# Wider first weight rows in contraction halves, with eight gate blocks of two columns held open in PSUM

## The chip, the cores and the metric

The kernel runs on one core of a Trainium2 chip. The metric is device time in microseconds (us) of one execution. Before the change the median is 178.38 us over six runs (178.31 to 178.41). The profiled execution of the kernel before was taken apart from the six, and took 178.62 us, and its span (first to last instruction) is about 1.7 us shorter than its device time.

Names: PE is the matrix engine and PEld its weight loads, DVE the vector engine, ACT the scalar engine, SP the engine that issues most transfers. Times "at 6.66" are us from the start of the span.

## The reference, cut to what matters

```python
# x [1, 2048, 512], w_gate and w_up [512, 1792], w_down [1792, 512], all bf16
xn = _layernorm(x, axis=-1)
A = irfft2(rfft2(xn) * (w_r + 1j * w_i))             # spectral branch
g = einsum("bsd,df->bsf", xn, w_gate)                # contraction over 512
u = einsum("bsd,df->bsf", xn, w_up)
B = einsum("bsf,fd->bsd", gelu(g) * u, w_down)
return x + A + B
```

The change touches only the first 14 us: loading x and the first columns of `w_gate` and `w_up`, and the first matmuls of g and u.

## The kernel before

The 2048 rows of x are 16 "columns" c of 128 rows. The 1792 columns of the weights are 14 blocks "fc" of 128. The contraction of 512 is four blocks e of 128. A "unit" computes gate and up for n columns and m blocks fc. For columns 0 and 1 the kernel wants to start before all weights are there, so its transfers and units are cut finely. The order of instructions is decided by a planner from keys and estimated times (`add(engine, duration, function, dependences, key=...)`).

The loads, in their order in the queue:

```python
pin(load_x(0, 1))                      # column 0 of x, 128 KB
pin(load_x(1, 1))
nc.sync.dma_start(out=idx_t[:], ...)   # a small index table, needed much later
load_w(Wg_sb, 0, 512)                  # 512 KB: fc 0-3, all four e; rows of 512 bf16 = 1 KB
load_w(Wu_sb, 0, 512)                  # 512 KB
load_x(2, 2)
for e in range(0, NE, 2):
    load_w(Wg_sb, 512, 1024, e=slice(e, e + 2))   # fc 4-7, two e at a time
load_w(Wu_sb, 512, 1024)
load_x(4, 4)
load_w(Wg_sb, 1024, DF)
...
```

Before the weights are there, PE spins: 37 matmuls of no use at the start, and 11 more after the transposes of column 0, meant to keep its clock up.

```python
for k in range(37):
    pin(nc.tensor.matmul(sp_ps[:, :P], lhsT=spin[:], rhs=spin[:], start=True, stop=True))
def spin_on():
    for k in range(11):
        nc.tensor.matmul(sp_ps[:, :P], lhsT=spin[:], rhs=x_t[:, 0, :P], start=True, stop=True)
```

The first units, `(first column, columns, first fc, fc)`, and the piecewise gate of the first of them:

```python
todo = [(0, 1, 0, 4), (1, 1, 0, 4), (0, 2, 4, 2), (0, 2, 6, 2)]
todo += [(2, 2, f, 2) for f in range(0, 8, 2)]
...
def mm_part(e0, e1):
    if e0 == 0:
        b["g_ps"] = ps.tile([P, m, w], F32, name="g_ps", tag="G", bufs=2)
    for e in range(e0, e1):
        for f in range(m):
            T_.matmul(b["g_ps"][:, f], lhsT=Wg_sb[:, e, (f0 + f) * P:(f0 + f + 1) * P],
                      rhs=rhs[:, e, :], start=(e + f == 0), stop=(e == NE - 1), ...)
...
if k == 0:
    g = add("PE", occ / 4, lambda: mm_part(0, 1), [xT_op[0, 0]], key=1000, ...)
    between["t", 0].deps.append(g)           # transposes of column 1 between the parts
    g = add("PE", occ / 4, lambda: mm_part(1, 2), [g, between["t", 1]], key=1000.1)
    g = add("PE", occ / 2, lambda: mm_part(2, NE), [xT_op[0], g], key=1000.2, ...)
```

So for fc 0 to 3 a landed piece of 512 KB feeds gate (or up) of column 0 and of column 1 over the whole contraction.

Of the kernel before, what the change touches and what calls it, by code (L numbers as in the profile page):

```python
# [10 lines left out]
P = 128  # L11
BF16 = mybir.dt.bfloat16
F32 = mybir.dt.float32
# [4 lines left out]
S = 2048  # L18
# [3 lines left out]
NE = 4  # L22
# [112 lines left out]
class Plan:  # L135
# [6 lines left out]
    def add(self, eng, occ, fn, deps=(), key=0.0, lat=None, slack=0.0, t_min=0.0, acq=(), rel=(), after=None):  # L142
        lat = occ + 0.25 if lat is None else lat
        op = Op(len(self.ops), eng, occ, lat, fn, [d for d in deps if d is not None], key, slack, t_min, acq, rel,
                after)
        self.ops.append(op)
        return op
# [54 lines left out]
def kernel(  # L202
# [24 lines left out]
    ps = ctx.enter_context(tc.tile_pool(name="ps", bufs=2, space=bass.MemoryType.PSUM))  # L227
    pw = ctx.enter_context(tc.tile_pool(name="pw", bufs=2))
# [3 lines left out]
    Wg_sb = pc.tile([P, NE, DF], BF16, name="Wg_sb")  # L232
    Wu_sb = pc.tile([P, NE, DF], BF16, name="Wu_sb")
# [19 lines left out]
    def load_x(c0, n, eng=nc.sync):  # L253
        eng.dma_start(out=x_t[:, c0:c0 + n, :], in_=x_v[:, c0:c0 + n, :])

    def load_w(a, b, eng=nc.sync):
        nc.sync.dma_start(out=Wg_sb[:, :, a:b], in_=wg_v[:, :, a:b])
        eng.dma_start(out=Wu_sb[:, :, a:b], in_=wu_v[:, :, a:b])
# [23 lines left out]
    pin(load_x(1, 1))  # L282
    idx_t = pc.tile([P, 3], I32, name="idx_t")
    nc.sync.dma_start(out=idx_t[:], in_=nc.inline_tensor(idx_np, name="spec_rows").ap())
    load_w(Wg_sb, 0, 512)
    load_w(Wu_sb, 0, 512)
    load_x(2, 2)
    for e in range(0, NE, 2):
        load_w(Wg_sb, 512, 1024, e=slice(e, e + 2))
    load_w(Wu_sb, 512, 1024)  # L290
    load_x(4, 4)
    load_w(Wg_sb, 1024, DF)
    load_w(Wu_sb, 1024, DF)
    load_x(8, 2)
# [10 lines left out]
        for h in range(2):  # L305
            nc.sync.dma_start(out=Tf[64 * h:64 * h + 64, W:8 * W], in_=rows[h, :, 0:4, W:8 * W])

    LAND = {0: 2.7, 1: 3.4, 2: 8.55, 3: 8.55}
    LAND.update({c: 11.5 if c < 8 else 17.5 if c < 12 else 20.5 for c in range(4, NC)})
    WG_LAND = [6.1] * 4 + [10.15] * 4 + [13.2] * 6  # L310
    WU_LAND = [7.6] * 4 + [11.7] * 4 + [15.2] * 6
    RF_LAND = 19.0

    ident = ident_t[:]
# [5 lines left out]
        pin(nc.tensor.matmul(sp_ps[:, :P], lhsT=spin[:], rhs=spin[:], start=True, stop=True))  # L320

    def spin_on():
        for k in range(11):
            nc.tensor.matmul(sp_ps[:, :P], lhsT=spin[:], rhs=x_t[:, 0, :P], start=True, stop=True)

    plan = Plan({"S": 4, "G": 2, "U": 2, "ge": 3, "A": 1, "xf": 2, "ds": 4, "E": 2, "X": 2, "Y": 2, "F": 2,
                 "F2": 3, "y_sb": 3})
    add = plan.add
    V, A, T_ = nc.vector, nc.scalar, nc.tensor
# [18 lines left out]
    def f_T(c, e0, n):  # L348
        tiles["T", c, e0] = tp = ps.tile([P, n, P], BF16, name="tp", tag="S", bufs=4)
        for e in range(n):  # L350
            T_.transpose(tp[:, e], xn[:, c, (e0 + e) * P:(e0 + e + 1) * P], ident)  # L351
# [20 lines left out]
    xn_op, xT_op, between = {}, {}, {}  # L372

    def first_two():
        o = {}

        def v(k, fn, occ, deps=(), lat=None, t_min=0.0):
            o[k] = add("DVE", occ, fn, [o[d] for d in deps], key=-2000 + len(o), lat=lat, t_min=t_min,
                       after=o.get("last"))
            o["last"] = o[k]  # L380

        def T(c, h):
            o["T", c, h] = add("PE", 0.12, lambda: f_T(c, 2 * h, 2), [o["xn", c, h]], key=-2000 + 2 * c + h,
                               lat=0.36, acq=("S",))

        def xn_(c, h):
            v(("xn", c, h), lambda: f_norm_v(c, 256 * h, 256), 0.27, [("recip", c)], lat=0.4)

        def stats(c):
            v(("stats", c), lambda: f_stats(c), 0.6, t_min=LAND[c], lat=0.7)  # L390

        def mean(c):
            v(("mean", c), lambda: f_mean(c), 0.17, [("stats", c)])
            o["root", c] = add("ACT", 0.31, lambda: A.activation(
                out=rstd[:, c:c + 1], in_=mv[:, c, 1:2], func=AF.Sqrt, bias=eps_t[:], scale=1.0),
                [o["mean", c]], key=-2000 + c)

        def recip(c):
            v(("recip", c), lambda: V.reciprocal(out=rstd[:, c:c + 1], in_=rstd[:, c:c + 1]), 0.15, [("root", c)])

        stats(0)
        mean(0)
        stats(1)

        recip(0)
        xn_(0, 0)
        mean(1)
        xn_(0, 1)
        T(0, 0)
        T(0, 1)  # L410
        add("PE", 0.61, spin_on, [o["T", 0, 1]], key=-1500, lat=0.61, after=o["T", 0, 1])
        table = add("ACT", 1.3, lambda: None, [o["root", 1]], key=-1500, lat=1.3)
        v("copy0", lambda: f_Tc(0, 0, 2), 0.25, [("T", 0, 0)], lat=0.4)
        o["copy0"].rel = ("S",)
        xT_op[0, 0] = o["copy0"]
        recip(1)
        v("copy1", lambda: f_Tc(0, 2, 2), 0.25, [("T", 0, 1)], lat=0.4)
        o["copy1"].rel = ("S",)
        xT_op[0] = o["copy1"]
        xn_op[0] = o["xn", 0, 1]  # L420
        v("xn1", lambda: f_norm_v(1, 0, D), 0.33, [("recip", 1)], lat=0.45)
        o["t", 0] = add("PE", 0.12, lambda: f_T(1, 0, 2), [o["xn1"]], key=1000.04, lat=0.3, acq=("S",))
        o["t", 1] = add("PE", 0.12, lambda: f_T(1, 2, 2), [o["xn1"]], key=1000.05, lat=0.3, acq=("S",),
                        after=o["t", 0])
        between.update(o)
        v("copyt0", lambda: f_Tc(1, 0, 2), 0.25, [("t", 0)], lat=0.4)
        o["copyt1"] = add("ACT", 0.4, lambda: f_Tc(1, 2, 2, A.copy), [o["t", 1], table], key=-1400)
        o["copyt0"].rel = o["copyt1"].rel = ("S",)
        xT_op[1, 0] = o["copyt0"]
        xT_op[1] = o["copyt1"]  # L430
        xn_op[1] = o["xn1"]
# [42 lines left out]
    def unit(k, c0, n, f0, m=1):  # L474
        sb, o, w = c0 // 4, (c0 % 4) * P, n * P
# [10 lines left out]
        b = {}  # L486
# [7 lines left out]
                    T_.matmul(b[name][:, f], lhsT=W_[:, e, (f0 + f) * P:(f0 + f + 1) * P], rhs=rhs[:, e, :],  # L494
                              start=(e == 0), stop=(e == NE - 1))

        def mm_part(e0, e1):
            if e0 == 0:
                b["g_ps"] = ps.tile([P, m, w], F32, name="g_ps", tag="G", bufs=2)
            for e in range(e0, e1):  # L500
                for f in range(m):
                    T_.matmul(b["g_ps"][:, f], lhsT=Wg_sb[:, e, (f0 + f) * P:(f0 + f + 1) * P], rhs=rhs[:, e, :],  # L502
                              start=(e + f == 0), stop=(e == NE - 1), skip_group_check=True)

        def f_ge():
            b["ge"] = pw.tile([P, m, w], BF16, name="ge", bufs=3)
            A.activation(out=b["ge"][:], in_=b["g_ps"][:], func=AF.Gelu_apprx_tanh)  # L507

        def f_h():
# [6 lines left out]
        def split(name, tag, W_, key, t, h):  # L516
            o = None
            for f in range(0, m, h):
                o = add("PE", occ * h / m, lambda f=f: mm(name, tag, W_, range(f, f + h)), [o] if f else src, key=key,
                        lat=occ * h / m + 0.3, acq=() if f else (tag,), t_min=t[f0 + f + h - 1])  # L520
            return o

        if k == 0:
            g = add("PE", occ / 4, lambda: mm_part(0, 1), [xT_op[0, 0]], key=1000, acq=("G",), t_min=WG_LAND[0])
            between["t", 0].deps.append(g)
            g = add("PE", occ / 4, lambda: mm_part(1, 2), [g, between["t", 1]], key=1000.1)
            g = add("PE", occ / 2, lambda: mm_part(2, NE), [xT_op[0], g], key=1000.2, lat=occ / 2 + 0.3)
        elif k < 4:
            late_half = WG_LAND[f0] + 0.05
            first = [xT_op[1, 0]] if k == 1 else src  # L530
            g = add("PE", occ / 2, lambda: mm_part(0, 2), first, key=1000 + k if k < 3 else 1002.2, acq=("G",),
                    t_min=late_half - (0.7 if k > 1 else 0.0))
            g = add("PE", occ / 2, lambda: mm_part(2, NE), [*src, g], key=1000.3 + k, lat=occ / 2 + 0.3, t_min=late_half)
        else:
            g = split("g_ps", "G", Wg_sb, 1000 + k, WG_LAND, m)
        u = split("u_ps", "U", Wu_sb, (1001.4, 1001.5, 1003.1, 1003.5)[k] if k < 4 else 1000.5 + k, WU_LAND, (2, m, 1)[k] if k < 3 else m)
        ge = add("ACT", {1: 0.28, 2: 0.36, 4: 0.5}[n * m], f_ge, [g], key=-1000 + k,
                 lat={1: 0.38, 2: 0.48, 4: 0.7}[n * m], acq=("ge",), rel=("G",))
        h = add("DVE", {1: 0.21, 2: 0.34, 4: 0.61}[n * m], f_h, [ge, u], key=-1000 + k, rel=("U", "ge"))
        for c in range(c0, c0 + n):  # L540
            for f in range(f0, f0 + m):
                h_op[c, f] = h

    todo = [(0, 1, 0, 4), (1, 1, 0, 4), (0, 2, 4, 2), (0, 2, 6, 2)]
    todo += [(2, 2, f, 2) for f in range(0, 8, 2)]
    todo += [(0, 4, f) for f in range(8, NFC)]
    todo += [(4 * sb, 4, f) for sb in range(1, NSB) for f in range(NFC)]
# [345 lines left out]
```

## Time and profile before

| reading | value | view |
|---|---|---|
| device time | 178.38 us | timed runs |
| PE busy | 172.8 us, 98% | page, part 1 |
| share of the waiting chain that is PE | 95% | page, part 4 |
| first gate matmul | 6.66 | timeline |
| first 256-wide unit (columns 2-3) | 14.49 | timeline |
| PE busy between these two | 7.83 of 7.83 us | windows |

From the page of the kernel before: its span, the busy time of each engine, PE's row of 40 slices in tenths, and the chain that ended last.

```profile
span 176.9 us, 3143 instructions
...
PE 172.8 (98%) x1150; PEld 96.9 (55%) x1150; DVE 115.9 (66%) x255; ACT 96.0 (54%) x171; POOL 17.2 (10%) x38
...
PE   7999999999999999999999999999999999999993
...
PE 95%; DVE 2%; DMA 1%; issue 0%
```

PE is the bound, with no weak slice but the first and the last. The timeline of PE and PEld, same kernel (start, duration in us, engine, line, operation; in brackets how long the engine sat idle before it and what ended that). The duration of a group runs to its last matmul's modelled end, so it overlaps the next group; use the starts.

```profile
5.86 0.78 PE L324 MATMUL sp_ps<-x_t,spin 128*128 128x128 bf16 x11
...
6.66 0.23 PEld L502 LDWEIGHTS <-Wg_sb 128*128 128x128 bf16 x4 [0.20 <-DMA Wg_sb<-in_B_w_gate_dram]
6.66 0.40 PE L502 MATMUL g_ps<-xnT,Wg_sb 128*128 128x128 bf16 x4
...
6.90 0.39 PE L351 MATMUL tp<-ident_t,xn 128*128 128x128 bf16 x4
...
7.12 1.73 PE L502 MATMUL g_ps<-xnT,Wg_sb 128*128 128x128 bf16 x28
...
8.69 1.95 PE L494 MATMUL u_ps<-xnT,Wu_sb 128*128 128x128 bf16 x32
...
10.47 1.91 PE L502 MATMUL g_ps<-xnT,Wg_sb 128*128 128x256 bf16 x16
...
12.22 0.69 PE L351 MATMUL tp<-ident_t,xn 128*128 128x128 bf16 x8
...
12.75 1.91 PE L494 MATMUL u_ps<-xnT,Wu_sb 128*128 128x256 bf16 x16
...
14.49 1.04 PE L494 MATMUL g_ps<-xnT,Wg_sb 128*128 128x256 bf16 x8
```

The first weight load waited 0.20 us, and what it waited for was the transfer of `w_gate`. After that there is no bracket at all. The windows view confirms it (window, its length, then busy us and instructions of PE, PEld, DVE, ACT and POOL, the granted clock, the DMA share and GB/s):

```profile
6.66:14.49 7.83, 7.83 (x108) 7.34 (x109) 4.75 (x12) 4.30 (x7) 0.97 (x2) 1.00 1.03 357
```

From the first 256-wide matmul (14.49) to the last matmul's start (173.93) is 159.44 us here. With what follows and what lies outside the span, the device time of this profiled run is the start of the 256-wide units plus 164.13 us (14.49 + 164.13 = 178.62, measured 178.62). This profiled run was slower than all six timed runs. By the same sum 178.38 us corresponds to a start at 14.25.

### The profile page before, as it was taken

The page shows a single profiled execution, that of the slowest core. Times are in us where ns is not written, and L with a number is a line of the kernel's source. Part 1 is how long each engine was busy: PE and PEld are TensorE (multiplying, and loading weights), DVE is VectorE, ACT ScalarE, POOL GpSimd, SP SyncE. Part 2 cuts the span into 40 slices and gives each one's busy share as a digit, 9 for nine tenths or more (in the row PEclk, how much of TensorE's full clock was granted, in tenths as well). Part 3 has the DMA queues.
Part 4 walks back from the last instruction along what each step waited for, and adds up shares of the span by engine and source line. Part 5 has one row for each costly group of instructions (what it writes and reads, how often), then busy time and mean ns, then how long its engine had stood idle before and what let it go on. Part 6 is the DMA issues. An engine that isn't in the chain of part 4 may idle for free.

```text
span 176.9 us, 3143 instructions
## 1 busy us (share of the span) xinstructions
PE 172.8 (98%) x1150; PEld 96.9 (55%) x1150; DVE 115.9 (66%) x255; ACT 96.0 (54%) x171; POOL 17.2 (10%) x38
## 2 busy tenths in 40 slices
PE   7999999999999999999999999999999999999993
PEld 7798845455545554555555455454445445444463
DVE  2588999987434599979899999643516325345333
ACT  3452489799736988898899965362112111211200
POOL 1020340506760000000000000000000000000000
DMA  3999999233717802211201510200122221221212
GB/s 99 323 387 377 371 199 151 60 64 71 246 41 238 299 0 59 59 30 35 59 19 42 152 47 15 59 0 4 59 89 89 77 75 60 89 88 60 82 40 59
DMA packets 21743, 19.35 MB, mean 109 GB/s; under 512 B 8480, under 2 KB 20000, under 8 KB 21728
## 3 DMA queue, kind: packets, MB, share of 16 engines
q1 hardware_dynamic: 21312, 17.84, 36.4%
q0 software_dynamic: 416, 1.32, 2.6%
q8 instruction: 9, 0.15, 0.4%
q14 instruction: 6, 0.05, 0.1%
HBM read 13.38 MB, written 2.10 MB: 87 GB/s over the span
## 4 chain that ended last, share of the span: by engine, by line
PE 95%; DVE 2%; DMA 1%; issue 0%
PE u_ps L494 27%; PE y_ps L829 27%; PE g_ps L494 25%; PE g_ps L502 2%; PE bp L589 2%; PE yp L780 2%; PE gp L750 2%; PE dp L647 2%; PE y_ps L833 2%; PE ep L656 2%; DMA x_t<-in_A_x_dram 1%; DVE stats L339 1%; PE tp L351 1%; DVE xn L345 0%; DVE xnT L354 0%; DVE y_sb L836 0%
## 5 line engine op out<-in xcount | busy, mean ns | idle before, releaser
L494 PE MATMUL u_ps<-xnT,Wu_sb 128*128 128x512 bf16 (+2 forms) x272 | 57.1, 341 | 0.0
L494 PE MATMUL g_ps<-xnT,Wg_sb 128*128 128x512 bf16 (+1 forms) x224 | 53.3, 364 | 0.0
L829 PE MATMUL y_ps<-Wd_sb,hT 128*128 128x512 bf16 (+2 forms) x252 | 51.1, 355 | 0.0
L512 DVE TENSOR_TENSOR hT<-u_ps,ge 128x512 bf16<-128x512 f32 x56 | 38.4, 688 | 18.1 <-PE u_ps L494 16.5
L507 ACT ACTIVATE ge<-g_ps 128x512 bf16<-128x512 f32 x56 | 33.5, 601 | 22.3 <-PE g_ps L494 18.3
L494 PEld LDWEIGHTS <-Wu_sb 128*128 128x128 bf16 x272 | 24.8, 98 | 20.7
L829 PEld LDWEIGHTS <-hT 128*128 128x128 bf16 x252 | 23.2, 98 | 22.4
L494 PEld LDWEIGHTS <-Wg_sb 128*128 128x128 bf16 x224 | 21.5, 98 | 20.5
L786 ACT CAST yf<-yp 128x512 bf16<-128x512 f32 x16 | 9.3, 586 | 40.5 <-PE yp L780 40.5
L836 DVE TENSOR_TENSOR y_sb<-y_ps,y_sb 128x512 bf16<-128x512 f32 (+2 forms) x18 | 11.1, 632 | 30.0 <-PE y_ps L833 30.0
L661 ACT CAST E<-ep 64x512 bf16<-64x512 f32 x32 | 18.5, 579 | 1.4 <-PE ep L656 1.0
L339 DVE BATCH_NORM_STATS2 stats<-x_t 128x6 f32<-128x512 bf16 x16 | 10.4, 674 | 3.9 <-DMA x_t<-in_A_x_dram 3.9
L456 ACT ACTIVATE xn<-x_t,nb,rstd 128x512 bf16<-128x512 bf16 x12 | 9.5, 812 | 1.0 <-POOL nb L370 1.0
L559 ACT CAST ds<-dp 128x512 bf16<-128x512 f32 x16 | 9.2, 597 | 0.8 <-PE dp L647 0.8
L559 ACT CAST Gs<-gp 128x512 bf16<-128x512 f32 x16 | 8.7, 591 | 0.6 <-PE gp L750 0.5
L559 ACT CAST Bs<-bp 128x512 bf16<-128x512 f32 x16 | 8.3, 606 | 0.5 <-PE bp L589 0.5
L792 DVE TENSOR_TENSOR lv<-yf 128x512 bf16<-128x512 bf16 x16 | 6.1, 421 | 1.5 <-ACT yf L786 0.6
L780 PEld LDWEIGHTS <-Gs 128*128 128x128 bf16 x64 | 4.8, 98 | 3.5
L799 DVE TENSOR_TENSOR yt<-lv 128x512 bf16<-128x512 bf16 x16 | 6.1, 421 | 0.3
L833 PE MATMUL y_ps<-yt,RI_t 128*128 128x512 bf16 (+2 forms) x18 | 6.1, 355 | 0.0
L780 PE MATMUL yp<-CT,Gs 128*128 128x128 bf16 x64 | 6.0, 219 | 0.0
L571 DVE TENSOR_TENSOR A<-xn 128x1024 bf16<-128x1024 bf16 x8 | 5.2, 676 | 1.0 <-ACT xn L456 1.0
(65 smaller groups left out, 125.5 us busy)
## 6 DMA issues: line engine op xcount, KB each, us to landing
F<-F SPq DMA_DIRECT2D x32, 64.0 KB, 2.0
y_sb<-in_A_x_dram SPq DMA_DIRECT2D x16, 128.0 KB, 2.1
out_dram<-y_sb SPq DMA_DIRECT2D x15, 128.0 KB, 1.7
Wd_sb<-in_B_w_down_dram SPq DMA_DIRECT2D x1, 1792.0 KB, 7.6
x_t<-in_A_x_dram SPq DMA_DIRECT2D x5, 256.0 KB, 9.8
Wu_sb<-in_B_w_up_dram SPq DMA_DIRECT2D x2, 512.0 KB, 6.2
Wg_sb<-in_B_w_gate_dram SPq DMA_DIRECT2D x1, 768.0 KB, 10.2
Wu_sb<-in_B_w_up_dram SPq DMA_DIRECT2D x1, 768.0 KB
```

Source lines behind the costliest of these rows:

```text
L339: V.bn_stats(out=st[:], in_=x_t[:, c, :])
L456: xn_op[c] = add("ACT", 0.72, lambda c=c: A.activation(out=xn[:, c, :], in_=x_t[:, c, :], func=AF.Identity, bias=nb[:, c:c + 1], scale=rst ...
L494: T_.matmul(b[name][:, f], lhsT=W_[:, e, (f0 + f) * P:(f0 + f + 1) * P], rhs=rhs[:, e, :], start=(e == 0), stop=(e == NE - 1))
L507: A.activation(out=b["ge"][:], in_=b["g_ps"][:], func=AF.Gelu_apprx_tanh)
L512: V.tensor_tensor(out=hT_of(sb, f0, m, o, w), in0=b["u_ps"][:], in1=b["ge"][:], op=ALU.mult)
L559: A.copy(out=o, in_=i)
L661: A.copy(out=b["E"][64 * h:64 * h + 64, r], in_=b["ep", h][64 * r:64 * r + 64])
L780: T_.matmul(t[:, q], lhsT=late["G"][:, q, c0 + j], rhs=IQ[q], start=(q == 0), stop=(q == 3), skip_group_check=True)
L786: A.copy(out=b["yf"][:, j], in_=b[j][:])
L829: T_.matmul(b[o][:], lhsT=hT_of(sb, f, 1, cl * P, P)[:, 0], rhs=Wd_sb[:, f, o:o + w], start=(f == 0), stop=False)
L833: T_.matmul(b[o][:], lhsT=late["RI"][:, c, :], rhs=late["yt"][:, c, o:o + w], start=False, stop=True)
L836: V.tensor_tensor(out=b["y"][:, o:o + w], in0=b[o][:], in1=b["y"][:, o:o + w], op=ALU.add)
```

## The change

Its intent: make the rows of the first weight transfers 2 KB wide in place of 1 KB, so that they move faster and the first half is there sooner; keep PE fed by holding the gate sums of columns 0 and 1 over eight fc open in four PSUM banks (the two of the gate pool and the two of the up pool) until the second half of the contraction is there; then run all of up. Cumulative bytes per transfer stay the same: 512 KB each. Six of the eleven spins go.

```diff
-    load_w(Wg_sb, 0, 512)
-    load_w(Wu_sb, 0, 512)
-    load_x(2, 2)
-    for e in range(0, NE, 2):
-        load_w(Wg_sb, 512, 1024, e=slice(e, e + 2))
-    load_w(Wu_sb, 512, 1024)
-    load_x(4, 4)
+    for T in (Wg_sb, Wu_sb):
+        for e in range(0, NE, 2):
+            load_w(T, 0, 1024, e=slice(e, e + 2))
+        if T is Wg_sb:
+            load_x(2, 2)
+    load_x(4, 2)
+    load_x(6, 2)
...
     def spin_on():
-        for k in range(11):
+        for k in range(5):
...
-        o["t", 0] = add("PE", 0.12, lambda: f_T(1, 0, 2), [o["xn1"]], key=1000.04, ...)
+        o["t", 0] = add("PE", 0.12, lambda: f_T(1, 0, 2), [o["xn1"]], key=1000.13, ...)
...
+        gt, ut = "G", "U"
+        if k < 4:
+            def parts(name, tag, W_, key, t):
+                o = None
+                for e in (0, 2):
+                    o = add("PE", occ / 2, lambda e=e: mm_part(name, tag, W_, e), [o] if o else [], ...)
+                    o.deps.append(xT_op[c0, 0] if e == 0 else xT_op[c0])
+                    if k == 1 and W_ is Wg_sb:
+                        between["t", 0].deps.append(o) if e == 0 else o.deps.append(between["t", 1])
+                return o
+            gt = ut = "GU"[k // 2]
+            g = parts("g_ps", gt, Wg_sb, 1000 + 0.1 * (k % 2) + 0.4 * (k // 2), (5.3, WG_LAND[0]))
+            u = parts("u_ps", ut, Wu_sb, 1001 + 0.1 * (k % 2) + 0.4 * (k // 2), (8.6, WU_LAND[0]))
...
-    todo = [(0, 1, 0, 4), (1, 1, 0, 4), (0, 2, 4, 2), (0, 2, 6, 2)]
+    todo = [(0, 1, 0, 4), (0, 1, 4, 4), (1, 1, 0, 4), (1, 1, 4, 4)]
     todo += [(2, 2, f, 2) for f in range(0, 8, 2)]
```

More of the change, by code (lines that the diff above doesn't have):

```diff
@@ L306 @@
             nc.sync.dma_start(out=Tf[64 * h:64 * h + 64, W:8 * W], in_=rows[h, :, 0:4, W:8 * W])
-    LAND = {0: 2.7, 1: 3.4, 2: 8.55, 3: 8.55}
+    LAND = {0: 2.7, 1: 3.4, 2: 7.2, 3: 7.2}
     LAND.update({c: 11.5 if c < 8 else 17.5 if c < 12 else 20.5 for c in range(4, NC)})
-    WG_LAND = [6.1] * 4 + [10.15] * 4 + [13.2] * 6
-    WU_LAND = [7.6] * 4 + [11.7] * 4 + [15.2] * 6
+    WG_LAND = [6.6] * 8 + [13.2] * 6
+    WU_LAND = [9.9] * 8 + [15.2] * 6
     RF_LAND = 19.0
@@ L322, in spin_on @@
     def spin_on():
-        for k in range(11):
+        for k in range(5):
             nc.tensor.matmul(sp_ps[:, :P], lhsT=spin[:], rhs=x_t[:, 0, :P], start=True, stop=True)
-    plan = Plan({"S": 4, "G": 2, "U": 2, "ge": 3, "A": 1, "xf": 2, "ds": 4, "E": 2, "X": 2, "Y": 2, "F": 2,
+    plan = Plan({"S": 4, "G": 2, "U": 2, "ge": 4, "A": 1, "xf": 2, "ds": 4, "E": 2, "X": 2, "Y": 2, "F": 2,
                  "F2": 3, "y_sb": 3})
@@ L410, in first_two @@
         T(0, 1)
-        add("PE", 0.61, spin_on, [o["T", 0, 1]], key=-1500, lat=0.61, after=o["T", 0, 1])
+        add("PE", 0.28, spin_on, [o["T", 0, 1]], key=-1500, lat=0.28, after=o["T", 0, 1])
         table = add("ACT", 1.3, lambda: None, [o["root", 1]], key=-1500, lat=1.3)
@@ L421, in first_two @@
         v("xn1", lambda: f_norm_v(1, 0, D), 0.33, [("recip", 1)], lat=0.45)
-        o["t", 0] = add("PE", 0.12, lambda: f_T(1, 0, 2), [o["xn1"]], key=1000.04, lat=0.3, acq=("S",))
-        o["t", 1] = add("PE", 0.12, lambda: f_T(1, 2, 2), [o["xn1"]], key=1000.05, lat=0.3, acq=("S",),
+        o["t", 0] = add("PE", 0.12, lambda: f_T(1, 0, 2), [o["xn1"]], key=1000.13, lat=0.3, acq=("S",))
+        o["t", 1] = add("PE", 0.12, lambda: f_T(1, 2, 2), [o["xn1"]], key=1000.14, lat=0.3, acq=("S",),
                         after=o["t", 0])
@@ L495, in mm, with mm_part @@
                               start=(e == 0), stop=(e == NE - 1))
-        def mm_part(e0, e1):
+        def mm_part(name, tag, W_, e0):
             if e0 == 0:
-                b["g_ps"] = ps.tile([P, m, w], F32, name="g_ps", tag="G", bufs=2)
-            for e in range(e0, e1):
+                b[name] = ps.tile([P, m, w], F32, name=name, tag=tag, bufs=2)
+            for e in (e0, e0 + 1):
                 for f in range(m):
-                    T_.matmul(b["g_ps"][:, f], lhsT=Wg_sb[:, e, (f0 + f) * P:(f0 + f + 1) * P], rhs=rhs[:, e, :],
+                    T_.matmul(b[name][:, f], lhsT=W_[:, e, (f0 + f) * P:(f0 + f + 1) * P], rhs=rhs[:, e, :],
                               start=(e + f == 0), stop=(e == NE - 1), skip_group_check=True)
         def f_ge():
-            b["ge"] = pw.tile([P, m, w], BF16, name="ge", bufs=3)
+            b["ge"] = pw.tile([P, m, w], BF16, name="ge", bufs=4)
             A.activation(out=b["ge"][:], in_=b["g_ps"][:], func=AF.Gelu_apprx_tanh)
@@ L521, in split @@
             return o
-        if k == 0:
-            g = add("PE", occ / 4, lambda: mm_part(0, 1), [xT_op[0, 0]], key=1000, acq=("G",), t_min=WG_LAND[0])
-            between["t", 0].deps.append(g)
-            g = add("PE", occ / 4, lambda: mm_part(1, 2), [g, between["t", 1]], key=1000.1)
-            g = add("PE", occ / 2, lambda: mm_part(2, NE), [xT_op[0], g], key=1000.2, lat=occ / 2 + 0.3)
-        elif k < 4:
-            late_half = WG_LAND[f0] + 0.05
-            first = [xT_op[1, 0]] if k == 1 else src
-            g = add("PE", occ / 2, lambda: mm_part(0, 2), first, key=1000 + k if k < 3 else 1002.2, acq=("G",),
-                    t_min=late_half - (0.7 if k > 1 else 0.0))
-            g = add("PE", occ / 2, lambda: mm_part(2, NE), [*src, g], key=1000.3 + k, lat=occ / 2 + 0.3, t_min=late_half)
+        gt, ut = "G", "U"
@@ new lines, in unit @@
+        if k < 4:
+            def parts(name, tag, W_, key, t):
+                o = None
+                for e in (0, 2):
+                    o = add("PE", occ / 2, lambda e=e: mm_part(name, tag, W_, e), [o] if o else [], lat=occ / 2 + 0.3,
+                            key=key + 0.1 * e, acq=() if o else (tag,), t_min=t[e // 2])
+                    o.deps.append(xT_op[c0, 0] if e == 0 else xT_op[c0])
[5 more added lines that the diff above has]
+            u = parts("u_ps", ut, Wu_sb, 1001 + 0.1 * (k % 2) + 0.4 * (k // 2), (8.6, WU_LAND[0]))
@@ L534, in unit @@
         else:
             g = split("g_ps", "G", Wg_sb, 1000 + k, WG_LAND, m)
-        u = split("u_ps", "U", Wu_sb, (1001.4, 1001.5, 1003.1, 1003.5)[k] if k < 4 else 1000.5 + k, WU_LAND, (2, m, 1)[k] if k < 3 else m)
+            u = split("u_ps", "U", Wu_sb, 1000.5 + k, WU_LAND, m)
         ge = add("ACT", {1: 0.28, 2: 0.36, 4: 0.5}[n * m], f_ge, [g], key=-1000 + k,
-                 lat={1: 0.38, 2: 0.48, 4: 0.7}[n * m], acq=("ge",), rel=("G",))
-        h = add("DVE", {1: 0.21, 2: 0.34, 4: 0.61}[n * m], f_h, [ge, u], key=-1000 + k, rel=("U", "ge"))
+                 lat={1: 0.38, 2: 0.48, 4: 0.7}[n * m], acq=("ge",), rel=(gt,))
@@ L540, in unit @@
+        h = add("DVE", {1: 0.21, 2: 0.34, 4: 0.61}[n * m], f_h, [ge, u], key=-1000 + k, rel=(ut, "ge"))
         for c in range(c0, c0 + n):
```

## The prediction

> **What bounds the kernel now.** TensorE. The page gives PE 98% busy, and the chain of waits is 95% PE. The windows view shows it busy 7.83 of 7.83 us from 6.66 to 14.49 us, and without a gap to 170 us; the timeline has it running to 174.15 us. No wait of PE appears after 6.66 us. Only three things can move the time: when the first gate matmul starts (6.66 us), how much work PE has after that, and holes that PE gets newly.
>
> **Why it starts at 6.66.** The timeline: the first gate weight load sat 0.20 us idle, put down to the DMA of Wg. The eleven spinning matmuls end at about 6.47, the first transposed half-column is copied by 6.03. So the weights decide, not the spins.
>
> **What the change does.**
> 1. The first transfer of Wg keeps its size (512 KB) and place, but has 256 rows of 2 KB in place of 512 of 1 KB. In the trace's DMA packet records a 1 KB packet takes 46 ns, a 2 KB packet 84 to 92, a 4 KB packet 159: 2 KB rows move 0 to 9% faster when all engines are fed. This agrees with the Trainium skill, "DMA: Bandwidth & Descriptors", section "Why small descriptors are slow", which has a fixed cost per packet. More to be had is in the ramp: from 3.25 to 5.0 us only about 344 packets of 1 KB start, where the later rate is 92 to 95 per quarter us; that loses about 0.8 us. If the supply of descriptors is the limit there, half as many descriptors give half of it back. Estimate: the first half lands at 6.1 us, not 6.6.
> 2. PE work after that: 32 matmuls of 256 columns (109 ns each) become 64 of 128 (55.7 ns): 3.50 to 3.57 us, +0.07 us. The six spins removed (0.33 us) free nothing unless the weights land before 6.4 us; with them gone PE could start at about 6.15.
> 3. New dependences. Gate of columns 0 and 1 over eight fc now runs before any up. Cumulative bytes of each transfer are the same as before, so at the old rate the landings would be 6.6 (gate, first half), 8.05 (second), 10.4 and 12.0 (up halves): PE would have 16 matmuls (0.89) and 4 transposes (0.22), wait 0.3 us, run 48 (2.67) to 10.7, 16 of up to 11.6, and wait 0.4 for the second up half: a loss of 0.6 us. With landings about 0.5 us earlier: start 6.15, waits of 0.2 and 0.2, the transposes of columns 2-3 (ready about 11.5 and 11.8) cost 0.1 to 0.2 more, and the 256-wide units start at about 14.35 rather than 14.49.
> 4. The up units reuse the gate banks after their gelu (table loaded at 9.0, gelu 0.54 us each): in time.
> 5. The order of the spectral matmuls among the later units is changed by the planner; DVE and ACT are 91 to 92% busy from 60 to 100 us (windows), so small PE holes (0 to 0.3 us) may come.
>
> **Result.** About 0.15 us gained: 178.2 us; 177.6 to 178.9. Within 2% almost surely, since the whole affair is under 1 us of 178.
>
> **What would show it.** First gate matmul at 6.1 to 6.3 us; holes of PE waiting for Wg near 7.3 and Wu near 11; 256-wide units from about 14.35; the same length from there to the end.
>
> **What would make it wrong.** The ramp is latency of first touches and not descriptors (then start stays 6.6 and time rises by 0.5 us); 2 KB rows with no stragglers (gain up to 0.5 us); planner-made holes between 60 and 120 us.

## The result, and the profile after

The median after is 178.81 us over six runs (178.61 to 178.96), against 178.38 (178.31 to 178.41) before. The ratio is 1.0022, interval 1.0009 to 1.0035: within 2%, slightly slower. (Every ratio here is the mean time of one kernel's runs over that of the other's of the same rounds, so it is not quite the ratio of the medians quoted beside it.) The prediction had 178.2 with a range of 177.6 to 178.9: the range held by 0.09 us, but the sign was wrong: 0.43 us lost where 0.15 were to be gained. The range held because it was wide enough for the loss that the prediction thought unlikely, and not because its gain came.

From the page of the changed kernel, the same lines as before without PE's row:

```profile
span 176.9 us, 3177 instructions
...
PE 171.2 (97%) x1158; PEld 96.6 (55%) x1176; DVE 115.6 (65%) x255; ACT 96.4 (55%) x171; POOL 16.7 (9%) x38
...
PE 94%; DMA 2%; issue 1%; SPq 1%; DVE 0%
```

Some matmul records are missing from this trace (1158 of PE against 1176 of PEld), so part of PE's lower busy time is not real. The share of DMA in the chain rose from 1 to 2%: the chain now begins with the weights rather than with x. The timeline of PE and PEld, changed kernel:

```profile
5.49 0.44 PE L324 MATMUL sp_ps<-x_t,spin 128*128 128x128 bf16 x5
...
6.45 0.90 PEld L502 LDWEIGHTS <-Wg_sb 128*128 128x128 bf16 x16 [0.69 <-DMA Wg_sb<-in_B_w_gate_dram]
6.45 1.07 PE L502 MATMUL g_ps<-xnT,Wg_sb 128*128 128x128 bf16 x16 [0.52 <-DMA Wg_sb<-in_B_w_gate_dram]
...
7.36 0.39 PE L351 MATMUL tp<-ident_t,xn 128*128 128x128 bf16 x4
...
7.77 2.68 PEld L502 LDWEIGHTS <-Wg_sb 128*128 128x128 bf16 x48 [0.20 <-DMA Wg_sb<-in_B_w_gate_dram]
7.77 2.85 PE L502 MATMUL g_ps<-xnT,Wg_sb 128*128 128x128 bf16 x48
...
10.46 1.50 PE L502 MATMUL u_ps<-xnT,Wu_sb 128*128 128x128 bf16 x24
...
11.80 0.61 PE L351 MATMUL tp<-ident_t,xn 128*128 128x128 bf16 x8
...
12.25 2.40 PE L502 MATMUL u_ps<-xnT,Wu_sb 128*128 128x128 bf16 x40
...
14.48 1.04 PE L494 MATMUL g_ps<-xnT,Wg_sb 128*128 128x256 bf16 x8
```

The first gate matmul starts at 6.45, after 0.69 us of waiting for the first half of the gate weights. At 7.77 there is a new hole: PEld waits 0.20 us for the second half. From 7.77 to 14.48 there is no other, 6.71 us of pure work. Matmuls of 128 columns follow each other every 55.7 ns, as before.

Mind which executions these are. This one (178.61 us) is the fastest of the changed kernel's six, and the trace of the kernel before is slower than all its timed runs, so the two traces start the 256-wide units alike (14.48 and 14.49). The medians differ by 0.43 us: by the sum above, 178.81 us is a start at 14.68, against 14.25 before.

The packet records of the two traces tell how fast the bytes came. When were the first 768 KB (as much as two columns of x and the first 512 KB of weights) through? And the first 1280 KB (with the second 512 KB of weights)? These are counts of bytes on the queue; the transfer that PE waits for reports its landing later, in the changed kernel at 6.41 for the first gate half.

```
kernel                            768 KB at   1280 KB at   2560 KB at
before                              5.51        6.92        10.97
changed                             5.39        6.70        10.50
median packet, ns: 1 KB 46; 2 KB 84 (changed)
median of the first 16 weight packets, ns: before 46; changed 624
first weight packet starts at: before 3.3; changed 3.28
```

In these two traces wide rows move bytes faster, by 0.12 us at the first half, 0.22 at the second and 0.47 at 2.5 MB. The gain that the prediction needed, 0.5 us at the first half, is not there: half as many packets did not shorten the ramp. Why the ramp is slow stays open. Most packets of 2 KB take 84 ns, but the first sixteen took 624 ns in the median here, which would fit the alternative that the prediction named as its own falsifier, a latency at the head. Later traces with the same first loads do not bear that out as the cause: there the median of the first sixteen was 403 (e2), 387 (e5), 138 (e11) and 122 ns (e9), and the two with quick first packets had their 768 KB no earlier (5.62 and 5.46). The Trainium skill, "DMA: Bandwidth & Descriptors", section "Latency and other measured facts", gives about 600 ns to the first byte for transfers that this engine issues; here the first weight packet (3.28) started 1.1 us after its issuing instruction did (2.18), but 0.6 us after that instruction was over (the next starts at 2.65), so the trace agrees if one counts from there.

### The profile page after: what moved, and what is told of

The parts are those of the page before. It is cut to its first block, busy times and chain, and to the rows that moved or that the text cites. A ratio compares the mean times of both kernels' runs of the same rounds, so it can differ in the third digit from the quotient of the medians. Undisturbed runs are those within 1.5% of the kernel's fastest.

```text
span 176.9 us, 3177 instructions
## 1 busy us (share of the span) xinstructions
PE 171.2 (97%) x1158; PEld 96.6 (55%) x1176; DVE 115.6 (65%) x255; ACT 96.4 (55%) x171; POOL 16.7 (9%) x38
## 4 chain that ended last, share of the span: by engine, by line
PE 94%; DMA 2%; issue 1%; SPq 1%; DVE 0%
PE y_ps L833 27%; PE g_ps L494 25%; PE u_ps L494 25%; DMA Wg_sb<-in_B_w_gate_dram 2%; PE g_ps L502 2%; PE yp L784 2%; PE dp L651 2%; PE gp L754 2%; PE u_ps L502 2%; PE bp L593 2%; PE y_ps L837 2%; PE ep L660 2%; SPq L273 0%; PE tp L351 0%; SPq L284 0%
## 5 line engine op out<-in xcount | busy, mean ns | idle before, releaser
L494 PE MATMUL u_ps<-xnT,Wu_sb 128*128 128x512 bf16 (+1 forms) x216 | 52.5, 364 | 0.3
L494 PEld LDWEIGHTS <-Wu_sb 128*128 128x128 bf16 x224 | 21.4, 98 | 20.2
L697 DVE TENSOR_TENSOR m<-X,TW 128x1024 bf16<-128x1024 bf16 x8 | 5.5, 688 | 0.2
```

The source lines that it names most:

```text
L494: T_.matmul(b[name][:, f], lhsT=W_[:, e, (f0 + f) * P:(f0 + f + 1) * P], rhs=rhs[:, e, :], start=(e == 0), stop=(e == NE - 1))
```

## The experiments

The theory after reading the two traces: the start of the 256-wide units is the latest of three times, namely first gate matmul + 7.82 us, second gate half landing + 6.71 us, second up half landing + 3.14 us (the work that PE still has after each). In the kernel before only the first bites, since its first 512 KB feed about 2 us of work (32 matmuls and 4 transposes). In the change the first 512 KB feed 16 matmuls and 4 transposes, 1.1 us, so PE catches up with the queue. Rivals: the six spins removed cost the time (clock or start); the wide rows themselves are at fault; or the planner moved holes into the rest of the kernel. The last one falls already: the stretch from the 256-wide units to the last matmul is 159.43 us after and 159.44 before.

Twelve kernels were run, four on a chip in each of three jobs, with five rounds, all correct by comparison. "Before" was 178.41 (178.03 to 178.65), 178.54 (177.99 to 178.99) and 178.78 (178.24 to 179.0) us in the three jobs, eleven runs each. Its spread of 0.6 to 1.0 us is wider than in the first measurement, so ratios and traces carry more here than single medians.

| run | what | median us | ratio to before, interval | first gate matmul | holes on PEld | 256-wide units |
|---|---|---|---|---|---|---|
| first measurement | before | 178.38 | | 6.66 | none | 14.49 |
| first measurement | changed | 178.81 | 1.0022 [1.0009, 1.0035] | 6.45 | 0.20 | 14.48 |
| e1_b_spin5 | before, 5 spins | 178.36 | 1.0005 [0.999, 1.0021] | 6.30 | 0.17 | 14.21 |
| e2_a_spin11 | changed, 11 spins | 178.72 | 1.0017 [1.0003, 1.003] | 6.02 | 0.33, 0.44 | 14.61 |
| e3_b_idx | e1 + index load late | 178.00 | 0.9983 [0.9969, 0.9996] | 5.70 | 0.35 | 13.79 |
| e4_a_idx | changed + index load late | 178.40 | 0.9999 [0.9985, 1.0013] | 5.67 | 1.03 | 14.52 |
| e5_a_c1first | changed, column 1 first | 178.84 | 1.0015 [0.9999, 1.0032] | 6.12 | 0.30, 0.48 | 14.74 |
| e6_a_idx_c1first | e5 + index load late | 178.34 | 0.9994 [0.9977, 1.0011] | 5.76 | 0.35 | 14.03 |
| e7_b_best | e3, other order, 3 spins | 178.26 | 0.9988 [0.9967, 1.0009] | 6.18 | none | 14.29 |
| e8_a_rows1k | changed, 1 KB rows | 179.91 | 1.0093 [1.006, 1.0126] | 6.01 | 0.74, 0.23, 0.48 | 15.51 |
| e9_a_nowait | changed, second halves not loaded | 179.02 | 1.0021 [1.0002, 1.0039] | 6.33 | none | 14.15 |
| e10_b_idx_again | e3 again | 178.26 | 0.9976 [0.9961, 0.9991] | 6.19 | 0.18 | 14.11 |
| e11_a_again | changed, unedited | 179.09 | 1.0029 [0.9996, 1.0061] | 6.88 | none | 16.33 |
| e12_b_best5 | e7 with 5 spins | 178.11 | 0.9966 [0.995, 0.9982] | 6.18 | none | 13.95 |

The trace columns are of the one profiled run of each kernel (the holes are those after the first gate matmul). That run need not be typical: it was the fastest of its six for the changed kernel and e3, and the slowest for e2 (178.77) and e4 (178.64).

### e1 and e2: the spins alone

```diff
 # e1, on the kernel before        # e2, on the changed kernel
-for k in range(11):               -for k in range(5):
+for k in range(5):                +for k in range(11):
```

> The kernel before with 5 spins in place of 11, nothing else. Theory W (the landing of the first gate weights sets the start of the first gate matmul; spins are only filler): first gate matmul still waits for the DMA, the hole before it grows by about 0.3 us, time within 0.1 us of before. Rival S (the spins hold the start in the usual run of before, since its profiled run was about 0.25 us slower than its timed runs): time falls by 0.2 to 0.35 us. The start also shows when 512 KB in 1 KB rows lands.

> The changed kernel with the 11 spins of before put back. Theory W: the spins end at about 6.1, before the gate weights land at 6.4; time within 0.1 us of the changed kernel (178.8). Rival: the 0.5 us hole of TensorE before the first gate matmul costs clock afterwards; then the time falls by 0.2 us or more. It is also a second trace of the changed kernel's transfers: first gate half lands at 6.3 to 6.6 again if that is no accident.

e1 measured 178.36 us, ratio 1.0005: taking the six spins from the kernel before makes no difference clear of noise. e2 measured 178.72 us, ratio 1.0017: giving them back to the changed kernel leaves it slower than before. Both came as the theory expected. The timelines show why. PE, e1:

```profile
6.30 0.40 PE L502 MATMUL g_ps<-xnT,Wg_sb 128*128 128x128 bf16 x4 [0.24 <-DMA Wg_sb<-in_B_w_gate_dram]
```

PE was idle for the weights instead of spinning, and started when they came. PE, e2:

```profile
6.02 1.06 PE L502 MATMUL g_ps<-xnT,Wg_sb 128*128 128x128 bf16 x16
...
7.45 2.85 PE L502 MATMUL g_ps<-xnT,Wg_sb 128*128 128x128 bf16 x48 [0.16 <-DMA Wg_sb<-in_B_w_gate_dram]
...
11.47 0.62 PE L502 MATMUL u_ps<-xnT,Wu_sb 128*128 128x128 bf16 x8 [0.27 <-DMA Wu_sb<-in_B_w_up_dram]
...
14.61 1.04 PE L494 MATMUL g_ps<-xnT,Wg_sb 128*128 128x256 bf16 x8
```

This execution started 0.43 us earlier than the changed kernel's profiled one (6.02 against 6.45) and still reached the 256-wide units later, at 14.61 against 14.48. The start bought nothing: both second halves were late, and 11.47 + 3.14 = 14.61. The spins are out as the cause of the typical loss.

### e3 and e4: the same gift to both kernels, an earlier start

The small index load sits in the queue before the weights and isn't needed until much later. It is moved behind the early weights, which brings the weights forward in both kernels.

```diff
 # e3 on e1, e4 on the changed kernel
-nc.sync.dma_start(out=idx_t[:], ...)     # before the first load_w
...
+nc.sync.dma_start(out=idx_t[:], ...)     # e3: before load_x(4, 4); e4: before load_x(4, 2)
```

> The kernel before with 5 spins and the 1.5 KB index load issued after the weights of columns 0 to 1023 instead of ahead of them. The first gate transfer is issued about 0.42 us earlier. Theory W: the first gate matmul starts 0.3 to 0.4 us earlier and the whole kernel ends as much earlier, 178.0 us. Rival (start held by the DVE chain of column 0, or by spins): no change.

> The changed kernel with the index load issued after the four weight transfers; instruction order on every other engine is the same. Theory W, with the loss being late weights only: start 0.3 to 0.4 us earlier and each later half too, time 178.4. If the extra loss over before came from something else after 14.5 us (planner order), the time would still sit 0.4 us above the same edit of before; the trace past 14.5 us tells: its length to the end should equal before's within 0.05 us.

e3 measured 178.00 us, ratio 0.9983, and e4 178.40, ratio 0.9999: both gained about 0.4 us on their parents (178.36 for e1; 178.81 for the changed kernel, in other rounds). The times came as expected. The first 768 KB were through at 5.07 and 5.04. PE, e3:

```profile
5.70 0.40 PE L502 MATMUL g_ps<-xnT,Wg_sb 128*128 128x128 bf16 x4
...
6.27 0.40 PE L351 MATMUL tp<-ident_t,xn 128*128 128x128 bf16 x4 [0.18 <-DVE xn L345]
...
13.79 1.04 PE L494 MATMUL g_ps<-xnT,Wg_sb 128*128 128x256 bf16 x8
```

PE, e4:

```profile
5.67 1.06 PE L502 MATMUL g_ps<-xnT,Wg_sb 128*128 128x128 bf16 x16
...
7.80 2.85 PE L502 MATMUL g_ps<-xnT,Wg_sb 128*128 128x128 bf16 x48 [0.85 <-DMA Wg_sb<-in_B_w_gate_dram]
...
14.52 1.04 PE L494 MATMUL g_ps<-xnT,Wg_sb 128*128 128x256 bf16 x8
```

In these traces the two kernels part. Against their parents' profiled runs the first matmul came 0.60 us earlier in e3 (6.30 to 5.70) and the 256-wide units 0.42 us earlier. In e4 it came 0.78 us earlier (6.45 to 5.67), and the 256-wide units did not move (14.48 to 14.52): the hole at the second gate half swallowed all of it, and 7.80 + 6.72 = 14.52. But this sets the slowest run of e4 against the fastest of its parent. In the medians the gift was worth as much to both, as expected if later pieces come earlier too: e4's 178.40 says by the sum that its typical run starts the 256-wide units at about 14.27, and no trace of such a run was taken. What e4's trace shows is how one execution can lose an early start at the second half, not that the changed kernel always does.

### e5 and e6: column 1 into the first piece

If the first 512 KB feed too little work before the second are needed, give them more: column 1 is transposed after 8 gate matmuls, and the first halves of all four open groups come before any second half. e6 adds the late index load. The edit, condensed (the chaining is told in a comment):

```diff
-o["t", 0] = add("PE", ..., key=1000.13, ...)
+o["t", 0] = add("PE", ..., key=1000.03, ...)
...
+if W_ is Wg_sb and k == 0 and e == 0:
+    between["t", 0].deps.append(o)              # transposes of column 1 after 8 gate matmuls
+    # gate parts then chained: e=0 of k 0 to 3, then e=2 of k 0 to 3
+between["T", 2].after = o                       # transposes of columns 2-3 after the second up part
```

> The changed kernel, same transfers, but column 1 is transposed after 8 gate matmuls, and its gate matmuls of the first contraction half run before the second half of either column; so the first 512 KB feed 32 matmuls and 4 transposes (2.0 us) instead of 16 and 4 (1.1 us). The transposes of columns 2-3 stand after 32 up matmuls so that they do not wait. Theory D (the changed order outruns its weights: 1.1 us of work per 512 KB, which take 1.3 us or more to arrive): the hole of 0.2 to 0.4 us before the second gate half goes; time falls 0.2 to 0.4 us below the changed kernel, to 178.4 or 178.5; from the 256-wide units to the last matmul 159.43 us as in all others. Rival (holes only moved: the up halves are late instead): time stays 178.7 to 178.8 and a hole of 0.2 to 0.5 us appears before the second up half.

> Both edits: index load late and column 1 first. In e4 the early start (5.67 us) was eaten by a hole of 0.85 us before the second gate half. Theory D: that hole goes, 256-wide units start at 13.7 to 13.9 and time is 177.9 to 178.1, level with e3. Rival: a hole of 0.4 us or more before the up halves, time 178.3 to 178.5.

e5 measured 178.84 us, ratio 1.0015; the expected gain missed. e6 measured 178.34, ratio 0.9994, where 177.9 to 178.1 was expected; it is the rival's time. PE, e5:

```profile
6.80 3.29 PE L503 MATMUL g_ps<-xnT,Wg_sb 128*128 128x128 bf16 x56
...
11.60 1.07 PE L503 MATMUL u_ps<-xnT,Wu_sb 128*128 128x128 bf16 x16 [0.31 <-DMA Wu_sb<-in_B_w_up_dram]
...
14.74 1.04 PE L495 MATMUL g_ps<-xnT,Wg_sb 128*128 128x256 bf16 x8
```

The hole at the second gate half is gone: 56 gate matmuls run in one piece from 6.80. But PE then waits for up: 0.30 us on PEld for the first up half at 10.22, and 0.31 on PE (0.48 on PEld) for the second at 11.60, and 11.60 + 3.14 = 14.74. The rival came true that the hole only moves. In e6 the one wait of that kind is shorter. PE, e6:

```profile
10.89 1.07 PE L503 MATMUL u_ps<-xnT,Wu_sb 128*128 128x128 bf16 x16 [0.18 <-DMA Wu_sb<-in_B_w_up_dram]
```

Here 10.89 + 3.14 = 14.03, which is where e6's 256-wide units start. Waits at two different halves in four traces (e2, e4, e5, e6), the last of them each time followed by just the work that PE had left, is what the theory asks for. It also says what is wrong in the layout: with a start at 6.45, the last half must be there by 6.45 + 7.82 - 3.14 = 11.13 if PE is not to stop, with 3.14 us of work behind it. In the kernel before the last 512 KB landed at about 12.0 (issued at 4.89, 7.1 us to landing), and are needed only at 12.75, with 1.74 us of work behind them.

### e8: the change with narrow rows

One transfer with 1 KB rows and the same bytes could not be built (the access pattern has too many dimensions), so each transfer is split in two.

```diff
-load_w(T, 0, 1024, e=slice(e, e + 2))
+load_w(T, 0, 512, e=slice(e, e + 2))
+load_w(T, 512, 1024, e=slice(e, e + 2))
```

> The changed kernel with each weight half as two transfers of 512 columns (1 KB rows again), nothing else; every other engine's order is the same. It gives up the wide rows and gains finer landing (8 gate matmuls can start on the first 256 KB). Theory L (slow first packets, not the number of descriptors, make the ramp): the bytes of the first half (768 KB in all) are through at 5.4 to 5.5 us as with wide rows, those of the second half 0.1 to 0.25 us later than with wide rows (6.9 against 6.7); time 178.7 to 179.0. If the number of descriptors limited the ramp: the 768 KB are through 0.3 us or more later than with wide rows and time rises by 0.3 to 0.6 us.

e8 measured 179.91 us (179.27 to 181.0), ratio 1.0093, worse than either expectation. The packet records of e8 put the first 768 KB through at 5.31, which is earlier than with wide rows (5.36 to 5.62 in the four traces of the change with the index load in its old place). So the first half shows no gain from wide rows. But the second came 0.69 us later (7.39 against 6.70), and there the test isn't clean: four more transfers had to be issued, and issuing the four of `w_gate` took SP 1.97 us in place of 0.94 for two. PE, e8 (its lines are numbered one higher):

```profile
7.98 3.09 PE L503 MATMUL g_ps<-xnT,Wg_sb 128*128 128x128 bf16 x48 [0.57 <-DMA Wg_sb<-in_B_w_gate_dram]
...
12.72 0.72 PE L352 MATMUL tp<-ident_t,xn 128*128 128x128 bf16 x8 [0.31 <-DVE xn L346]
```

The late bytes became a hole of 0.57 us, and later there was one of 0.31 us before the transposes of columns 2-3, whose normalisation was late. With its extra issues this run cannot by itself acquit the wide rows. The packet records do: in the bulk a packet of 2 KB takes 84 ns where two of 1 KB take 92, and in the four traces of the change with the old index load 2560 KB were through at 10.50 to 10.78, against 10.97 before. How much wide rows gain after the first half stays open.

### e9: no second halves to wait for

```diff
-for e in range(0, NE, 2):
-    load_w(T, 0, 1024, e=slice(e, e + 2))
+load_w(T, 0, 1024, e=slice(0, 2))
+nc.gpsimd.memset(T[:, 2:NE, 0:1024], 0.0)
```

> Wrong result on purpose: the changed kernel, but the second contraction half of the gate and up weights of columns 0 to 1023 is not loaded; GpSimd sets it to zero early. Instruction order on TensorE, VectorE and ScalarE is that of the changed kernel. This takes away the wait for the second halves (and 1 MB of traffic before x of columns 4-7). Theory D (all of the loss but 0.07 us is waiting for weights): no hole after the first gate matmul, which starts at 6.1 to 6.4 as before; 256-wide units start 7.8 to 7.9 us after it, at 14.0 to 14.3; time 178.2 to 178.45, level with or a little under before of the same rounds, 0.3 to 0.5 under the changed kernel (e11). Rival (the order itself costs, by PSUM banks freed late by gelu, or by the transposes of columns 2-3): holes of 0.3 us or more stay and time stays at 178.7 or over.

Half of the contraction of eight fc is zero here. (The comparison still passed it, so that comparison is blind to an error of this size in this branch.) In the first line PE's bracket names xn, while PEld's names the weights for the same moment; both were there at 6.28. PE, e9:

```profile
6.33 1.07 PE L502 MATMUL g_ps<-xnT,Wg_sb 128*128 128x128 bf16 x16 [0.41 <-DVE xn L345]
...
7.45 2.84 PE L502 MATMUL g_ps<-xnT,Wg_sb 128*128 128x128 bf16 x48
...
11.47 0.61 PE L351 MATMUL tp<-ident_t,xn 128*128 128x128 bf16 x8
11.92 2.40 PE L502 MATMUL u_ps<-xnT,Wu_sb 128*128 128x128 bf16 x40
14.15 1.04 PE L494 MATMUL g_ps<-xnT,Wg_sb 128*128 128x256 bf16 x8
```

The trace does what the theory said: no hole, and 7.82 us from first gate matmul to 256-wide units. The kernel before takes 7.83, but 0.08 of that is a stall in its transposes of columns 2-3 (its eight take 0.53 us from start to start, 12.22 to 12.75, where e9's take 0.45, 11.47 to 11.92). The narrower matmuls do cost what the prediction put down: 32 of 256 columns at 109 ns are 3.49 us, 64 of 128 at 55.7 ns are 3.56. Beside these 0.07 us and its waits the new order of work costs nothing in this trace. The timed result did not follow: 179.02 us, ratio 1.0021. Its six spans average 176.95 us against 177.02 for the kernel before of the same rounds, but 2.1 us of its device time lie outside the span, where all the others have 1.7. Why is open, and the timed result is not used further: that the typical loss goes with the waits is read from the traces, and no timed run shows it.

### e7, e10 and e12: towards a version that beats both

e7 takes e3 and removes its hole before the transposes of column 1: column 1 is normalised before the second copy of column 0, 8 gate matmuls run before those transposes, and the spins go down to 3. e12 is the same with 5 spins, and e10 repeats e3.

```diff
 # e7 on e3; e12 the same without the change of spins
-for k in range(5):
+for k in range(3):
...
+v("xn1", lambda: f_norm_v(1, 0, D), ...)          # now ahead of copy1 on DVE
 v("copy1", ...)
-v("xn1", lambda: f_norm_v(1, 0, D), ...)
...
-g = add("PE", occ / 4, lambda: mm_part(0, 1), ...)
+g = add("PE", occ / 2, lambda: mm_part(0, 2), ...)
...
+between["u0"].after = g                           # first up after gate of column 1
```

> The kernel before with the index load late, 3 spins, the normalisation of column 1 ahead of the second copy of column 0, and column 1's transposes after 8 gate matmuls in place of 4. In e3 TensorE started at 5.70 but lost 0.2 to 0.3 us waiting for column 1's normalised rows. Expected: first gate matmul 5.6 to 5.7, that hole gone, 256-wide units at about 13.5, time 177.65 to 177.8; faster than before by about 0.65 us (0.4%). If the weights land only at 5.9 in some runs, 177.9.

> e3 once more (the kernel before, index load late, 5 spins), to see whether its 0.4 us holds on another chip and against before of the same rounds: 178.0 to 178.2, 0.3 to 0.45 under before.

> e7 with 5 spins in place of 3. In e7 the profiled run had the weights late (6.18) and eight gate matmuls at 98 ns, so its clock was still half. If that was chance, time is 0.1 to 0.2 under e10 of the same rounds (hole before column 1's transposes gone), 177.8 to 178.0. If the transposes' place brings nothing, level with e10.

e7 measured 178.26 us, ratio 0.9988, and missed its expected 177.65 to 177.8. e10 measured 178.26, ratio 0.9976 on a chip where before was 178.78: a little over its expected time, and its gain on before held. e12 measured 178.11, ratio 0.9966, which is 0.15 us under e10 of the same rounds, as expected, though above the expected 177.8 to 178.0. PE, e12:

```profile
6.18 0.61 PE L502 MATMUL g_ps<-xnT,Wg_sb 128*128 128x128 bf16 x8
...
6.65 0.40 PE L351 MATMUL tp<-ident_t,xn 128*128 128x128 bf16 x4
...
13.95 1.04 PE L494 MATMUL g_ps<-xnT,Wg_sb 128*128 128x256 bf16 x8
```

There is no hole, and 7.77 us of work. In e7's trace the same 8 matmuls started 102 ns apart in the mean (6.18 to 7.00), where 55.7 is usual, and PE had waited 0.20 us for weights before them; that may be the price of two spins fewer, but it is one trace each. e12 beats both kernels: 0.34% under before with an interval clear of 1, and in the same rounds its slowest run (178.28) is under the fastest of the changed kernel (178.53, e11).

### e11: the changed kernel once more

> The changed kernel, unedited, in the same rounds as the others: 178.7 to 178.9, 0.3 to 0.5 over before. In the trace the 256-wide units start at whichever is later: first gate matmul + 7.85, landing of the second gate half + 6.7, landing of the second up half + 3.1.

Unedited, it measured 179.09 us against 178.78, ratio 1.0029: the same direction and size as at first, though the interval, 0.9996 to 1.0061, includes 1. But two of six executions took 180.46 and 180.62, and the profiled run was one of those. (e8 has two such runs as well, 181.0 and 180.99; no trace of either was taken.) The expected start of the 256-wide units, 6.88 + 7.85 = 14.73, missed by 1.6 us. PE, e11:

```profile
6.88 1.89 PE L502 MATMUL g_ps<-xnT,Wg_sb 128*128 128x128 bf16 x16 [0.61 <-DMA Wg_sb<-in_B_w_gate_dram]
...
8.99 3.48 PE L502 MATMUL g_ps<-xnT,Wg_sb 128*128 128x128 bf16 x48
```

The 16 matmuls started 105 ns apart (6.88 to 8.56), where 55.7 is usual, and the rate doubled only at 10.27. Some 32 matmuls at 107 ns in place of 56 are the missing 1.6 us. The Trainium skill, "TensorE: Matmul & The Clock Gate", section "Wait — 56ns, not 53.3ns?", gives 106.7 ns for the cold and 55.6 for the warm clock, which is what the trace shows. The windows of this run do not show it in the clock column (the last but two), which reads 1.00 in both, because this trace holds no record of the clock:

```profile
8.00:8.50 0.50, 0.50 (x8) 0.50 (x6) 0.00 (x0) 0.00 (x0) 0.00 (x0) 1.00 0.99 320
11.00:11.50 0.50, 0.50 (x13) 0.50 (x11) 0.00 (x0) 0.50 (x2) 0.42 (x2) 1.00 1.06 410
```

Eight matmuls in half a microsecond against thirteen: the count tells the clock. The section "What's actually happening" of the same page has full clock after about 3.4 us of sustained work in a window that runs freely; here it came 3.4 us after PE's restart (6.88 to 10.27), which fits, but 4.9 us of spins and transposes before the wait (1.05 to 5.96) had not brought it. In the other thirteen traces the rate doubled between 3.8 and 7.0. The last spin started at 5.96 and the first gate matmul at 6.88; at 107 ns each the six spins removed would have filled 0.64 us of that. That they would have saved these two executions is argued, not shown: e2, with all eleven, had no time above 178.77, but on another chip and in other rounds.

## Why the prediction was right or wrong

**The bound: right.** The time is the start of the 256-wide units plus a constant, 164.13 us, in twelve of fourteen traces.

**Step 1, an earlier first half (0.5 us): failed in size.** It took the slow ramp as a shortage of descriptors, to be halved by wider rows, and put the landing at 6.1 in place of 6.6. The first gate half landed at 6.41 in the changed kernel, and at 5.84, 6.08 and 6.83 in three more traces with these loads (e2, e5, e11); in the kernel before with equal spins (e1) it landed at 6.25. The first 768 KB came 0.12 us earlier (5.39 against 5.51), and with 1 KB rows in the change (e8, 5.31) no later than with wide ones. The prediction had named the case that start stays and the time rises by 0.5, and gave it too little weight; measured: 0.43. But the missing gain is not what turned the sign: e2 started at 6.02, before the predicted 6.15, and still reached the 256-wide units only at 14.61.

**Step 2, work on PE: right.** The 0.07 us for narrower matmuls is there (3.56 us in place of 3.49); in the traces compared, a stall of 0.08 us in the transposes of the kernel before hides it. The six spins free nothing in a typical run (e1). That they might also guard the clock was not considered; whether they do is open (e11).

**Step 3, new waits of 0.2 and 0.2: the mechanism right, the sum wrong, and this is the step that turned the sign.** The waits came where they were forecast: 0.20 at the second gate half in the profiled changed kernel, 0.33 and 0.44 in e2, 0.30 and 0.48 (both at up) in e5, all on PEld. But the prediction let them shrink to 0.2 and 0.2 while it moved the start earlier. Its own landings do not give that. With every landing 0.5 us earlier the second up half comes at 11.5, and with the 3.14 us of work left after it the 256-wide units start at 14.64, not 14.35; plus 164.13 that is 178.77 us, where 178.81 was measured. An earlier start only lengthens the wait, because the 256-wide units hang on the last landing plus the work behind it. Measured, the second up half landed at 11.23 in the changed kernel and at 11.42, 11.56 and 11.70 in e2, e5 and e11, about where the prediction's 11.5 would have it. The transposes of columns 2-3, put down at 0.1 to 0.2, cost nothing in the changed kernel's trace.

**Step 4, banks in time: right.** No trace of the change has PE waiting for a gelu.

**Step 5, holes from the planner: none.** The rest of the kernel is 159.43 and 159.44 us.

The split of the 0.43 us between start and waits differs between executions (0.20 of waiting at a start of 6.45, 0.77 at 6.02) and is not settled for the median, since no trace has the median's time.

## What to carry to other kernels

When the head of a kernel is fed by a queue, write for each transfer its landing time plus the work that is left after it; the latest sum decides, and an earlier first piece is worth nothing if a later piece has the latest sum. Order the work so that each landed piece feeds as much as it can before the next is needed: the contraction halves left PE with 1.1 us of work for its first 512 KB in place of 2.0. Wider rows helped the bulk of the stream (0.2 to 0.5 us at 2.5 MB) and not clearly its head; a small load that isn't needed yet, moved out of the queue's head (e3, e4), gained both kernels about 0.4 us.

## What the Trainium skill lacked or had wrong

- "DMA: Bandwidth & Descriptors", section "Why small descriptors are slow": the fixed cost per packet agrees with the bulk here (46 ns for 1 KB, 84 for 2 KB, 159 for 4 KB), but the section says nothing of a transfer's first packets. The first sixteen weight packets of 2 KB took 122 to 624 ns in the median in five traces with the same first loads (changed, e2, e5, e9, e11), and wider rows did not shorten the ramp.
- Same page, section "Latency and other measured facts": it has about 600 ns to the first byte and does not say from when. From the start of the issuing instruction it is 1.0 us here (x in the kernel before, 0.80 to 1.82) and 1.1 us (weights), from its end 0.6 us in both.
- "TensorE: Matmul & The Clock Gate", section "What's actually happening": the page calls the ramp penalty under 1% of a typical span. Two of six executions of e11 took 180.46 and 180.62 us, 1.6 us more than the mean of the other four (178.9), and the trace of the first shows a late full clock: 0.9%, so the figure holds, yet it is four times the effect under study here. The warning in the page's section "Seeing it yourself", that clock events in a trace can be unreliable, is not tested here: e11's trace has no such events at all, and the view's column reads 1.00 where none is recorded. In e7, which has them, full clock is recorded from 6.98, and its matmuls go from 107 to 56 ns apart between 6.90 and 7.00.
- Same page, "Part 4: PE-mode transpose", says that the full clock does not engage for transposes; four 128x128 transposes here took 0.22 us (6.90 to 7.12 in the kernel before), 55 ns each from start to start, so among matmuls, once the clock is up, they run at full rate. Whether transposes alone would bring the clock up no run tests.
